# Batch 0's opening reordered, and eight PSUM banks for the first h phase, in a fused attention and Gelu MLP kernel

## Chip, core and metric

One core of a Trainium2 chip. The metric is the device time of one execution in microseconds (us); medians of several runs are given. The profile comes from one of these executions; its span is about 1.8 us shorter than the metric (279.0 for 280.8). In the lines, PE is TensorE, PEld its weight loads, ACT ScalarE, DVE VectorE and POOL GpSimd; the granted clock is the share of TensorE's full clock that it was given.

## The reference, cut to what matters

```python
# q, k, v: (8, 8, 576, 64) float32; w_in: (512, 2048); w_out: (2048, 512)
q_s = softmax(q, over d)                    # per row
k_s = softmax(k, over the sequence)
kv  = einsum('bhsd,bhse->bhde', k_s, v)     # 64 x 64 for each head
x   = einsum('bhsd,bhde->bhse', q_s, kv)    # -> (4608, 512)
h   = x @ w_in
out = gelu(h) @ w_out                       # Gelu with erf; (4608, 512) float32
```

Per batch ("chunk") the kernel makes 512 rows of x, then h = x·w_in in 16 tiles t of 128 columns (four matmuls each, one for each slice dm of x), Gelu, and y = g·w_out. The rest of each batch's rows form a ninth chunk.

## The kernel before: the parts concerned

PSUM has eight banks, in three pools: psum_h (three single banks), psum_y (two), psum_a (one single, tag "a", and one pair, tag "a2"). A pool hands its banks out in turn, and a bank comes free when its last reader has finished. The names in the profile lines: `eq` (shown as `e`) is exp(q), `qT` its transpose, `ek` exp(k), `v_aug` v in bfloat16 with a column of ones, `kvc` the normalised kv, `xT` x in bfloat16, `g` Gelu's output.

```python
    warm(5, zeros32)                     # matmuls with zeros, to have the PE clock up
    table(AF.Exp)
    exp_q(0, parts=2); exp_k(0, parts=2)
    norm_q(0, 0, 2)                      # first half: multiply on POOL
    norm_q(0, 1, 2, nc.vector)           # second half: multiply on DVE
    tp_mm(0, 0); tp_evac(0, 0, "s")      # "s": evacuated by ACT, else by DVE
    table(AF.Gelu)
    warm(2)
    cast_v(0, 0)                         # DVE
    for hp in range(1, HP): cast_v(0, hp, nc.gpsimd)
    cast_wi(0, wi[0], "p"); cast_wi(1, wi[1], "p")    # POOL
    tp_mm(0, 1)
    warm(2)
    # ... x_tile: x0, x1 in psum_y, x2 in psum_a, x3 in psum_h
    kv_mm(0, 0); kv_norm(0, 0, 1)        # kv of heads 0-3, then its normalisation on DVE
    tp_evac(0, 1)
    warm_x()
    x_mm(0, 0); x_evac(0, 0, "s"); x_evac(0, 1, "s")
    kv_mm(0, 1); kv_norm(0, 1, 2)        # kv of heads 4-7
    x_mm(0, 1); x_evac(0, 2); x_evac(0, 3, "s")
    h_phase(0, {...}, groups={0: 2, 4: 4, 8: 2}, ybanks=(6, 8))
```

`groups={4: 4}` computes tiles 4 to 7 side by side: dm is the outer loop, so a late slice of w_in is wanted later. `ybanks` are the tiles that take a psum_y bank. The kv tile of a batch, both halves in the same pair of banks:

```python
            st[b]["kv"] = psum_a.tile([128, 2, 2, 256], FP32, tag="a2", name="kv")
        # matmul into ps[c, i, half, 0:D + 1]: i picks the bank, half the columns in it
```

The softmax here doesn't subtract the row's maximum and nothing guards it: scores larger than these inputs give would overflow.

Of the kernel before, what the change touches and what calls it, by code (L numbers as in the profile page):

```python
# [8 lines left out]
FP32 = mybir.dt.float32  # L9
BF16 = mybir.dt.bfloat16  # L10
AF = mybir.ActivationFunctionType
# [5 lines left out]
def kernel(  # L17
# [16 lines left out]
    nc = tc.nc  # L34
# [4 lines left out]
    M = 128 * J  # L39
    R = S - M  # L40
    HP = H // 2
# [11 lines left out]
    psum_h = ctx.enter_context(tc.tile_pool(name="psum_h", bufs=3, space=bass.MemoryType.PSUM))  # L53
    psum_y = ctx.enter_context(tc.tile_pool(name="psum_y", bufs=2, space=bass.MemoryType.PSUM))
    psum_a = ctx.enter_context(tc.tile_pool(name="psum_a", bufs=1, space=bass.MemoryType.PSUM))
# [14 lines left out]
    zeros32 = singles.tile([128, 512], FP32)  # L70
    scr = singles.tile([128, 2], FP32)

    def setup_tiles():
        nc.vector.memset(scr, 0.0)
        for i in range(2):
            nc.vector.memset(v_aug[i][:, :, :, D:D + 1], 1.0)

    def table(func):
        nc.scalar.activation(out=scr[:, 1:2], in_=scr[:, 0:1], func=func)  # L79
# [76 lines left out]
    def cast_v(b, hp, eng=nc.vector):  # L156
        eng.tensor_copy(  # L157
            out=v_aug[b % 2][:, hp, :, 0:D],
            in_=st[b]["vf"][:, hp, :].rearrange("p (n d) -> p n d", n=NS),
        )  # L160
# [5 lines left out]
    def kv_mm(b, half):  # L166


        if "kv" not in st[b]:
            st[b]["kv"] = psum_a.tile([128, 2, 2, 256], FP32, tag="a2", name="kv")  # L170
        ps = st[b]["kv"]
        for n in range(NS):
            for i in range(2):
                for hh in range(2):
                    hp = 2 * half + i
                    pr = slice(hh * 64, hh * 64 + 64)
                    c = slice((hh ^ i) * 64, (hh ^ i) * 64 + 64)
                    nc.tensor.matmul(  # L178
                        ps[c, i, half, 0:D + 1], ek[b % 2][pr, hp, n, :],
                        v_aug[b % 2][pr, hp, n, 0:D + 1], start=(n == 0), stop=(n == NS - 1),  # L180
                    )

    def kv_norm(b, h0, h1):

        ps = st[b]["kv"]
        m = h1 - h0
        rec = small.tile([128, 2, 2], FP32, tag="reck")
        nc.vector.reciprocal(rec[:, :, 0:m], ps[:, :, h0:h1, D])
        nc.vector.tensor_tensor(  # L189
            out=kvc[b].rearrange("p (h i) d -> p i h d", i=2)[:, :, h0:h1],  # L190
            in0=ps[:, :, h0:h1, 0:D],
            in1=rec[:, :, 0:m].unsqueeze(3).to_broadcast([128, 2, m, D]), op=ALU.mult,
        )
# [21 lines left out]
    def tp_mm(b, half):  # L215
        if half == 0:
            st[b]["qT"] = attn_sb.tile([128, J, HP, 128], BF16, tag="qT", name="qT")
        if b == 1 and half == 1:
            ps = psum_a.tile([128, 2, J, 2, 128], BF16, tag="a2", name="tp")[:, 0]
        else:  # L220
            pool, tag = (psum_h, "h") if half == 1 else (psum_a, "a")
            ps = pool.tile([128, J, 2, 128], BF16, tag=tag)
        st[b][f"tp{half}"] = ps
        for i in range(2):
            hp = 2 * half + i
            for j in range(J):
                nc.tensor.transpose(  # L227
                    ps[:, j, i, :],
                    st[b]["eq"][:, j, 2 * hp:2 * hp + 2, :].rearrange("p h d -> p (h d)"),
                    identity,  # L230
                )

    def tp_evac(b, half, eng="v"):
        o = st[b]["qT"][:, :, 2 * half:2 * half + 2, :]
        if eng == "v":
            nc.vector.tensor_copy(out=o, in_=st[b][f"tp{half}"])
        else:
            nc.scalar.copy(out=o, in_=st[b][f"tp{half}"])  # L238
# [17 lines left out]
    def x_mm(b, half):  # L256

        for bb in range(B if b == B else 1):
            for r in range(2):
                for i in range(2):  # L260
                    hp = 2 * half + i
                    pr = slice(r * 64, r * 64 + 64)
                    c = slice((r ^ i) * 64, (r ^ i) * 64 + 64)
                    ps = st[b][f"x{hp}"]
                    if b < B:
                        nc.tensor.matmul(  # L266
                            ps[c, :], kvc[b][pr, hp, :], st[b]["qT"][pr, :, hp, :],
                            start=True, stop=True,
                        )
                    else:  # L270
                        nc.tensor.matmul(  # L271
                            ps[c, bb * R:(bb + 1) * R], kvc[bb][pr, hp, :],
                            st[b]["qT"][pr, bb // 2, hp, bb % 2 * R:(bb % 2 + 1) * R],
                            start=True, stop=True,
                        )
# [11 lines left out]
    def x_evac(b, hp, eng="v"):  # L287
        ps = st[b][f"x{hp}"]
        if eng == "v":
            nc.vector.tensor_copy(out=st[b]["xT"][:, hp, :], in_=ps)  # L290
        else:
            nc.scalar.copy(out=st[b]["xT"][:, hp, :], in_=ps)  # L292

    def h_phase(c, ins, groups={}, ybanks=()):


        g = moe_sb.tile([128, NDF, M], BF16, tag="g", bufs=1)
        st[c]["g"] = g
        xT = st[c]["xT"]
        t1 = 0  # L300
        while t1 < NDF:
            t0, t1 = t1, t1 + groups.get(t1, 1)
            ts = range(t0, t1)
            pss = []
            for t in ts:
                pool, tag = (psum_y, "y") if t in ybanks else (psum_h, "h")
                pss.append(pool.tile([128, M], FP32, tag=tag, name="ps"))
            for dm in range(NDM):
                for ps, t in zip(pss, ts):
                    nc.tensor.matmul(  # L310
                        ps, wi_bf[:, dm, t * 128:(t + 1) * 128], xT[:, dm, :],
                        start=(dm == 0), stop=(dm == NDM - 1),
                    )
            for ps, t in zip(pss, ts):
                nc.scalar.activation(out=g[:, t, :], in_=ps, func=AF.Gelu)  # L315
                for f in ins.get(t, []):
                    f()
# [68 lines left out]
    def cast_wi(i, w, eng):  # L386
        n = wi_cols[i]
        r = n // 128
        o = wi_bf[:, :, wi_off[i]:wi_off[i] + n].rearrange("p d (c m) -> p d c m", c=r)
        w = w[:, :, 0:n].rearrange("p d (m c) -> p d c m", c=r)  # L390
        if eng == "p":
            for h in range(2):
                nc.gpsimd.tensor_copy(out=o[:, 2 * h:2 * h + 2], in_=w[:, 2 * h:2 * h + 2])
        else:
            for c in range(NDM):
                nc.vector.tensor_copy(out=o[:, c], in_=w[:, c])  # L396
# [22 lines left out]
    def cast_wo(i, w, c0=0, n=4, eng="v"):  # L419
        o, w = wo_bf[:, 4 * i + c0:4 * i + c0 + n, :], w[:, c0:c0 + n]  # L420
        if eng == "v":
            nc.vector.tensor_copy(out=o, in_=w)  # L422
        else:
            nc.scalar.copy(out=o, in_=w)

    def warm(n, z=zeros):
        ps = psum_y.tile([128, DM], FP32, tag="y")
        for i in range(n):
            nc.tensor.matmul(ps, z[:, 0:128], z, start=True, stop=True)  # L429

    def warm_x():

        for r in range(2):
            for i in range(2):
                pr = slice(r * 64, r * 64 + 64)
                c = slice((r ^ i) * 64, (r ^ i) * 64 + 64)
                nc.tensor.matmul(
                    st[0][f"x{i}"][c, :], zeros[pr, 0:64], zeros[pr, :], start=True, stop=True,
                )
# [23 lines left out]
    nc.vector.memset(zeros32, 0.0)  # L463
    nc.vector.memset(zeros, 0.0)
    setup_tiles()
    warm(5, zeros32)


    table(AF.Exp)
# [3 lines left out]
    norm_q(0, 1, 2, nc.vector)  # L473
    tp_mm(0, 0)
    tp_evac(0, 0, "s")
    table(AF.Gelu)
    warm(2)
    cast_v(0, 0)
    for hp in range(1, HP):
        cast_v(0, hp, nc.gpsimd)  # L480
    cast_wi(0, wi[0], "p")
    cast_wi(1, wi[1], "p")
    tp_mm(0, 1)
    warm(2)
    for hp, pool, tag in ((0, psum_y, "y"), (1, psum_y, "y"), (2, psum_a, "a"), (3, psum_h, "h")):
        x_tile(0, hp, pool, tag)
    kv_mm(0, 0)
    kv_norm(0, 0, 1)
    tp_evac(0, 1)
    warm_x()  # L490
    x_mm(0, 0)
    x_evac(0, 0, "s")
    x_evac(0, 1, "s")
    kv_mm(0, 1)
    kv_norm(0, 1, 2)
    x_mm(0, 1)
    x_evac(0, 2)
    x_evac(0, 3, "s")
    h_phase(0, {
        0: [lambda: cast_wi(2, wi[2], "v")],  # L500
        2: [lambda: cast_wi(3, wi[3], "v")],
        6: [lambda: cast_wi(4, wi[4], "v")],
        9: [lambda: cast_wo(0, wo[0])],
        12: [lambda: cast_wo(1, wo[1])],
    }, groups={0: 2, 4: 4, 8: 2}, ybanks=(6, 8))


    exp_q(1, parts=2)
# [68 lines left out]
    for c in range(2, B + 1):  # L577
        nb = c + 2
        ins = {}
# [53 lines left out]
```

## Time and profile before

| | before |
|---|---|
| time, first three runs | 280.81 us (280.76 to 280.87) |
| PE's share of the chain that ended last | 93% |
| first transposes on PE | 9.98 us |
| kv of half 0 / of half 1 starts | 12.12 / 13.45 us |
| first h matmul (tile 0) | 14.92 us |
| first y matmul | 28.94 us |

Read the timeline from the first h matmul backwards. Everything after it is one nearly unbroken stream of matmuls, one every 0.216 us, so a change of the opening is worth what it moves that first matmul, plus the holes that it takes out of or puts into the stream. The lines themselves stand in the prediction. About one matmul in seventy is missing from the trace (1894 records, 1922 weight loads); such a gap is exactly two steps (0.432) and is no hole.

### The profile page before, as it was taken

What the parts mean: (1) busy time and instruction counts of PE and PEld (TensorE: products, weight loads), DVE (VectorE), ACT (ScalarE), POOL (GpSimd) and SP (SyncE); (2) the same over time, 40 slices, a digit from 0 to 9 for tenths busy, and PEclk for the clock granted to TensorE, in tenths of its full rate; (3) what the DMA queues carried; (4) which work ended last, traced back from release to release, by engine and by line L of the source; (5) the groups of instructions that cost most, each with busy time, mean ns of one, the idle gap of its engine ahead of it and who ended that gap; (6) DMA issues with size and microseconds to landing.
All of it is one profiled execution on the core that took longest, in us unless ns stands there. A gap on an engine that the chain in (4) does not pass through costs nothing.

```text
span 279.0 us, 4537 instructions
## 1 busy us (share of the span) xinstructions
PE 269.0 (96%) x1894; PEld 125.7 (45%) x1922; DVE 99.8 (36%) x151; ACT 158.0 (57%) x245; POOL 33.9 (12%) x26
## 2 busy tenths in 40 slices
PE   7689999999999999999999999999999999999995
PEld 3334454444444444444444444444444444444443
DVE  2766574309753530083007500651015200130012
ACT  4857766689377816691569346943683263136400
POOL 1720060002020130005000500050005000000000
PEclk9999999999999999999999999999999999999999
DMA  7999999962994139812991199117501500120033
GB/s 252 398 385 432 396 399 407 400 247 72 265 381 78 40 108 256 314 39 72 237 366 44 40 215 389 48 66 186 117 0 75 150 2 0 75 78 0 0 78 76
DMA packets 44980, 50.10 MB, mean 180 GB/s; under 512 B 20384, under 2 KB 29856, under 8 KB 44704
## 3 DMA queue, kind: packets, MB, share of 16 engines
q1 hardware_dynamic: 44560, 49.39, 53.5%
q10 hardware_dynamic: 400, 0.43, 0.5%
q8 instruction: 15, 0.25, 0.3%
q14 instruction: 5, 0.04, 0.1%
HBM read 36.70 MB, written 9.44 MB: 165 GB/s over the span
## 4 chain that ended last, share of the span: by engine, by line
PE 93%; DMA 2%; ACT 1%; issue 1%; POOL 1%; DVE 0%; SPq 0%
PE ps L310 45%; PE ps L320 43%; DMA f<-in_q_dram 2%; PE kv L178 2%; PE ps L266 2%; PE ps L345 1%; POOL e L210 1%; ACT L79 0%; ACT e L145 0%; PE ps L227 0%; ACT qT L238 0%; PE ps L271 0%; SPq L90 0%; PE tp L227 0%; PE xx L266 0%
## 5 line engine op out<-in xcount | busy, mean ns | idle before, releaser
L310 PE MATMUL ps<-xT,wi_bf 128*128 128x512 bf16 x565 | 125.6, 379 | 0.6
L320 PE MATMUL ps<-wo_bf,g 128*128 128x512 bf16 x543 | 122.1, 379 | 1.6 <-issue 1.1
L315 ACT ACTIVATE g<-ps 128x512 bf16<-128x512 f32 x144 | 85.2, 597 | 67.9 <-PE ps L310 67.8
L310 PEld LDWEIGHTS <-wi_bf 128*128 128x128 bf16 x576 | 56.1, 98 | 68.4 <-issue 1.1
L320 PEld LDWEIGHTS <-g 128*128 128x128 bf16 x560 | 54.0, 98 | 64.2 <-issue 0.4
L328 DVE COPY y_sb<-ps 128x512 f32<-128x512 f32 x34 | 23.2, 684 | 79.8 <-PE ps L320 76.8
L210 POOL TENSOR_TENSOR e<-e,recq 128x2048 bf16<-128x2048 bf16 (+1 forms) x9 | 25.7, 2856 | 177.8 <-DVE recq L209 143.0
L157 DVE CAST v_aug<-f 128x576 bf16<-128x576 f32 x25 | 17.1, 745 | 48.2 <-DMA f<-in_v_dram 48.2
L208 DVE TENSOR_REDUCE qsum<-e 128x16 f32<-128x1024 bf16 (+1 forms) x13 | 21.1, 1621 | 15.3 <-ACT e L145 15.2
L292 ACT CAST xT<-ps 128x512 bf16<-128x512 f32 x19 | 10.3, 589 | 26.5 <-PE ps L266 17.0
L145 ACT ACTIVATE e<-f 128x512 bf16<-128x512 f32 (+1 forms) x42 | 20.5, 556 | 2.9 <-DMA f<-in_q_dram 2.8
L150 ACT ACTIVATE ek<-f 128x2304 bf16<-128x2304 f32 (+1 forms) x10 | 17.1, 1726 | 0.4 <-DMA f<-in_k_dram 0.4
L290 DVE CAST xT<-ps 128x512 bf16<-128x512 f32 x15 | 9.7, 687 | 17.4 <-PE ps L266 14.6
L79 ACT ACT_TABLE_LOAD x9 | 11.5, 1283 | 2.8 <-issue 2.6
L429 PE MATMUL ps<-zeros 128*128 128x512 f32 (+1 forms) x14 | 8.0, 716 | 1.5 <-DVE zeros L463 1.5
L145 ACT ACT_TABLE_LOAD x7 | 9.0, 1283 | 0.1
L396 DVE CAST wi_bf<-w 128x512 bf16<-128x512 f32 x12 | 7.1, 623 | 2.1 <-DMA w<-in_moe_w_in_dram 1.7
L178 PEld LDWEIGHTS <-ek 64*64 64x64 bf16 x576 | 6.5, 105 | 2.5 <-ACT qT L238 0.4
L178 PE MATMUL kv<-v_aug,ek 64*64 64x65 bf16 x576 | 6.8, 193 | 0.0
L210 DVE TENSOR_TENSOR e<-e,recq 128x1024 bf16<-128x1024 bf16 x4 | 6.1, 1533 | 0.1
L266 PE MATMUL ps<-qT,kvc 64*64 64x512 bf16 x60 | 5.0, 390 | 1.0 <-DVE kvc L189 0.6
L422 DVE CAST wo_bf<-w 128x2048 bf16<-128x2048 f32 (+1 forms) x4 | 4.4, 1091 | 3.8 <-DMA w<-in_moe_w_out_dram 3.8
(37 smaller groups left out, 44.6 us busy)
## 6 DMA issues: line engine op xcount, KB each, us to landing
out_dram<-y_sb SPq DMA_DIRECT2D x32, 256.0 KB, 2.4
f<-in_k_dram SPq DMA_DIRECT2D x6, 1152.0 KB, 10.2
f<-in_v_dram SPq DMA_DIRECT2D x6, 1152.0 KB, 11.7
f<-in_q_dram SPq DMA_DIRECT2D x6, 1024.0 KB, 7.4
w<-in_moe_w_in_dram SPq DMA_DIRECT2D x6, 512.0 KB, 8.9
f<-in_v_dram SPq DMA_DIRECT2D x8, 288.0 KB, 6.8
f<-in_q_dram SPq DMA_DIRECT2D x4, 512.0 KB, 9.0
w<-in_moe_w_out_dram SPq DMA_DIRECT2D x2, 1024.0 KB, 12.2
```

Source lines behind the costliest of these rows:

```text
L79: nc.scalar.activation(out=scr[:, 1:2], in_=scr[:, 0:1], func=func)
L145: nc.scalar.activation(out=dst[:, i], in_=src[:, u], func=AF.Exp)
L150: nc.scalar.activation(out=ek[b % 2][:, i:i + n], in_=st[b]["kf"][:, i:i + n].rearrange("p x (n d) -> p x n d", n=NS), func=AF.Exp,)
L157: eng.tensor_copy(out=v_aug[b % 2][:, hp, :, 0:D], in_=st[b]["vf"][:, hp, :].rearrange("p (n d) -> p n d", n=NS),)
L178: nc.tensor.matmul(ps[c, i, half, 0:D + 1], ek[b % 2][pr, hp, n, :], v_aug[b % 2][pr, hp, n, 0:D + 1], start=(n == 0), stop=(n == NS - 1),)
L208: nc.vector.reduce_sum(out=qsum, in_=eq[:, :, hs, :], axis=AX.X)
L210: eng.tensor_tensor(out=eq[:, :, hs, :], in0=eq[:, :, hs, :], in1=recq.unsqueeze(3).to_broadcast([128, J, w, D]), op=ALU.mult,)
L266: nc.tensor.matmul(ps[c, :], kvc[b][pr, hp, :], st[b]["qT"][pr, :, hp, :], start=True, stop=True,)
L310: nc.tensor.matmul(ps, wi_bf[:, dm, t * 128:(t + 1) * 128], xT[:, dm, :], start=(dm == 0), stop=(dm == NDM - 1),)
L315: nc.scalar.activation(out=g[:, t, :], in_=ps, func=AF.Gelu)
L320: nc.tensor.matmul(ps, st[c]["g"][:, t, j * 128:(j + 1) * 128], wo_bf[:, t, :], start=(t == 0), stop=(t == NDF - 1),)
L328: nc.vector.tensor_copy(out=y_sb, in_=ps)
```

## The change

Its intent: have kv of both halves done before x, so that PE need not go back and forth between PE and DVE; give v's casts and the evacuations to the engines so that each piece is ready in turn; load Gelu's table when the last evacuation is done; and give the first h phase enough banks to compute tiles 4 to 7 and 8 to 11 side by side. `warm(7)` takes the place of `warm(5)`, and a later `warm(2)` goes.

```diff
@@ -463,7 +462,7 @@
     nc.vector.memset(zeros32, 0.0)
     nc.vector.memset(zeros, 0.0)
     setup_tiles()
-    warm(5, zeros32)
+    warm(7, zeros32)
 
 
     table(AF.Exp)
@@ -473,36 +472,51 @@
     norm_q(0, 1, 2, nc.vector)
     tp_mm(0, 0)
     tp_evac(0, 0, "s")
-    table(AF.Gelu)
     warm(2)
-    cast_v(0, 0)
-    for hp in range(1, HP):
-        cast_v(0, hp, nc.gpsimd)
+    cast_v(0, 0, nc.gpsimd)
+    cast_v(0, 1, nc.gpsimd)
+    cast_v(0, 2)
+    cast_v(0, 3, nc.gpsimd)
     cast_wi(0, wi[0], "p")
     cast_wi(1, wi[1], "p")
     tp_mm(0, 1)
-    warm(2)
+    tp_evac(0, 1, "s")
     for hp, pool, tag in ((0, psum_y, "y"), (1, psum_y, "y"), (2, psum_a, "a"), (3, psum_h, "h")):
         x_tile(0, hp, pool, tag)
     kv_mm(0, 0)
     kv_norm(0, 0, 1)
-    tp_evac(0, 1)
     warm_x()
+    kv_mm(0, 1)
+    kv_norm(0, 1, 2)
     x_mm(0, 0)
     x_evac(0, 0, "s")
-    x_evac(0, 1, "s")
-    kv_mm(0, 1)
-    kv_norm(0, 1, 2)
+    x_evac(0, 1)
     x_mm(0, 1)
-    x_evac(0, 2)
-    x_evac(0, 3, "s")
+    x_evac(0, 2, "s")
+    x_evac(0, 3)
+    table(AF.Gelu)
+
+    def ybank():
+        return psum_y.tile([128, M], FP32, tag="y", name="ps")
+
+    pair = []
+
+    def a2bank(i):
+        if not pair:
+            pair.append(psum_a.tile([128, 2, M], FP32, tag="a2", name="pair"))
+        return pair[0][:, i]
+
     h_phase(0, {
         0: [lambda: cast_wi(2, wi[2], "v")],
         2: [lambda: cast_wi(3, wi[3], "v")],
         6: [lambda: cast_wi(4, wi[4], "v")],
         9: [lambda: cast_wo(0, wo[0])],
         12: [lambda: cast_wo(1, wo[1])],
-    }, groups={0: 2, 4: 4, 8: 2}, ybanks=(6, 8))
+    }, groups={0: 2, 4: 4, 8: 4}, banks={
+        3: ybank, 6: ybank, 8: ybank,
+        9: lambda: psum_a.tile([128, M], FP32, tag="a", name="ps"),
+        10: lambda: a2bank(0), 11: lambda: a2bank(1),
+    })
 
 
     exp_q(1, parts=2)
```

The cut hunks replace the argument `ybanks` by `banks`, a map from a tile to a function that allocates its bank.

More of the change, by code (lines that the diff above doesn't have):

```diff
@@ L292, in x_evac, with h_phase @@
             nc.scalar.copy(out=st[b]["xT"][:, hp, :], in_=ps)
-    def h_phase(c, ins, groups={}, ybanks=()):
+    def h_phase(c, ins, groups={}, banks={}):
         g = moe_sb.tile([128, NDF, M], BF16, tag="g", bufs=1)
@@ L305, in h_phase @@
             for t in ts:
-                pool, tag = (psum_y, "y") if t in ybanks else (psum_h, "h")
-                pss.append(pool.tile([128, M], FP32, tag=tag, name="ps"))
+                pss.append(banks[t]() if t in banks else psum_h.tile([128, M], FP32, tag="h", name="ps"))
             for dm in range(NDM):
```

## The prediction

> **What bounds the kernel now.** I read the page first (busy shares, clock row, chain by line), then the timelines of each engine over the first 45 us, then the waits.
>
> ```profile
> PE 269.0 (96%) x1894; PEld 125.7 (45%) x1922; DVE 99.8 (36%) x151; ACT 158.0 (57%) x245; POOL 33.9 (12%) x26
> PEclk9999999999999999999999999999999999999999
> PE 93%; DMA 2%; ACT 1%; issue 1%; POOL 1%; DVE 0%; SPq 0%
> ```
>
> The reader is to see that TensorE (PE) holds 93% of the chain that ended last, at full clock. The change touches only the opening, before batch 0's first matmul with w_in, and the first h phase. All else it can do is let the same stream of matmuls start earlier or lose a hole, so the gain is at most a few us of 280.81. The timelines (columns: start, duration, engine, line, operation, tiles, shapes, count, idle before and releaser) show the opening:
>
> ```profile
> 9.98 0.62 PE L227 MATMUL ps<-identity,e 128*128 128x128 bf16 x8 [1.71 <-POOL e L210]
> 11.15 0.61 PE L227 MATMUL ps<-identity,e 128*128 128x128 bf16 x8
> 12.12 0.48 PE L178 MATMUL kv<-v_aug,ek 64*64 64x65 bf16 x36
> 13.21 0.41 PE L266 MATMUL ps<-qT,kvc 64*64 64x512 bf16 x4 [0.40 <-ACT scr L79]
> 14.58 0.41 PE L266 MATMUL ps<-qT,kvc 64*64 64x512 bf16 x4 [0.62 <-DVE kvc L189]
> 14.92 14.19 PE L310 MATMUL ps<-xT,wi_bf 128*128 128x512 bf16 x62
> ...
> 11.67 1.28 ACT L79 ACT_TABLE_LOAD   x1
> ...
> 12.87 0.29 DVE L189 TENSOR_TENSOR kvc<-kv,rec 128x128 bf16<-128x128 f32 x1
> ...
> 9.54 1.46 DVE L210 TENSOR_TENSOR e<-e,recq 128x1024 bf16<-128x1024 bf16 x1
> 10.93 0.74 DVE L157 CAST v_aug<-f 128x576 bf16<-128x576 f32 x1
> 8.02 1.90 POOL L210 TENSOR_TENSOR e<-e,recq 128x1024 bf16<-128x1024 bf16 x1 [6.71 <-ACT e L145]
> 10.41 2.34 POOL L157 CAST v_aug<-f 128x576 bf16<-128x576 f32 x3 [0.49 <-DMA f<-in_v_dram]
> 13.23 2.58 POOL L393 CAST wi_bf<-w 128x512 bf16<-128x512 f32 x4 [0.48 <-DMA w<-in_moe_w_in_dram]
> ```
>
> From 9.98 to 14.92 PE does little and waits on short chains: transposes of q, kv of half 0, its normalisation, x of half 0, then the same for half 1. The h phase starts at 14.92 and the y phase at 28.94: 64 tile-steps in 14.02 us. The wait "ACT scr L79" is a coincidence of ends: the table's dummy activation ends at 12.96 + 0.20, kvc at 12.87 + 0.29, both 13.16, and kvc is what x needs. There is one true hole inside the h phase:
>
> ```profile
> 15.58 1.03 PE L310 MATMUL ps<-xT,wi_bf 128*128 128x512 bf16 x4
> ...
> 18.38 1.22 PE L310 MATMUL ps<-xT,wi_bf 128*128 128x512 bf16 x4
> ...
> 18.58 0.60 ACT L315 ACTIVATE g<-ps 128x512 bf16<-128x512 f32 x1 [0.27 <-PE ps L310]
> ```
>
> Four matmuls take 1.03 at the steady pace (three steps of 0.216 and a last one of 0.379) and 1.22 here. The fourth is w_in tile 7's first. Counting the psum_h rotation (three buffers: transposes, x3, tiles 0, 1, 2, 3, 4, 5, 7), tile 7 takes tile 3's bank, whose Gelu ends at 18.58 + 0.60 = 19.18. The hole is 0.19 us.
>
> **What the Trainium skill says.** "GPSIMD Engine Reference", section 8, says that GpSimd shares its SBUF interfaces with VectorE and contends with DVE instructions that have two SBUF inputs. The trace agrees: DVE's normalising multiply took 1.46 us beginning at 9.54, while POOL's ran until 9.92, but 1.23 in a later place where they hardly overlap; and POOL's three v casts take 2.34 us at 10.41 where three take 2.06 at 38.83. I read it as turns: DVE's multiply works from 9.92 to 11.00, and a POOL cast given before that gets going only at 11.00.
>
> "PSUM — Partial Sum Buffer", section "PSUM bank collisions raise a hardware error", says two engines may not touch one bank in the same partitions at once and that hardware does not arbitrate, so software must order them. The kv tile holds half 0 and half 1 in the same two banks. That such ordering is in this program, even wider, by whole tile, is suggested here:
>
> ```profile
> 45.51 0.69 DVE L290 CAST xT<-xx 128x512 bf16<-128x512 f32 x1 [0.20 <-PE xx L266]
> 46.23 0.59 ACT L292 CAST xT<-xx 128x512 bf16<-128x512 f32 x1 [0.82 <-DVE xT L290]
> ```
>
> ACT reads the other half of one PSUM tile only after DVE has finished.
>
> "ScalarE: Activation LUTs", section "What ACT_TABLE_LOAD costs", gives about 1283 ns plus a drain of about 1380. The trace shows 1.28 and 0.20 for the dummy call, and no such drain: I use 1.48.
>
> **The change part by part.**
>
> 1. *warm(7) for warm(5).* Ten passes end at 1.45 + 6.82 = 8.27. Later passes step by about 0.43, so four more add 1.7 us and end at 9.98, the last one's successor being issuable at about 9.4. The transposes wait for POOL until 9.98. Cost 0.
>
> 2. *v casts.* v0, v1, v3 go to POOL, v2 to DVE. POOL is free at 9.92 instead of 10.41 (it no longer waits for v1's landing), but the port belongs to DVE until 11.00. v0 then ends near 11.53, v1 near 12.14, v3 near 12.75: just when POOL's three ended before (10.41 + 2.34 = 12.75). kv of half 0 needs v0 and v1, so it starts at 12.14 + 0.04 = 12.18, against 12.12. The warm(2) taken out stood in a gap that the casts now leave anyway. Worth −0.06 (a loss).
>
> 3. *kv of half 1 ahead of x.* From kv's start to the end of kvc took 12.12 to 13.16, 1.04 us; so kvc half 0 is ready at 13.23. By the bank rule kv of half 1, which writes those banks, waits for it: it starts at 13.26 and its kvc is ready at 14.30. x of half 0 is issued behind it at about 13.6 and seen done 0.45 later, 14.06. ACT evacuates x0 from 14.07 to 14.66 (its 0.59). DVE evacuates x1 behind kvc, 14.23 to 14.92 (0.69). x of half 1 waits for kvc, 14.35, seen done 14.80; x2 on ACT to 15.40, x3 on DVE to 15.53.
>
> 4. *Start of the h phase.* Tiles 0 and 1 are a pair, each needing a slice of x every 0.43 us. PE is past x of half 1 at 14.35 + 0.34 = 14.70 (14.58 to 14.92 before), x0 is there at 14.66, the first w_in cast (13.23 plus half of 1.3) long before. So h starts at 14.70, and x1 (needed 15.13), x2 (15.56), x3 (16.00) are in time. Worth 14.92 − 14.70 = 0.22.
>
> 5. *tp_evac of half 1 on ACT* costs 1.01 there instead of 0.68 on DVE; it runs 11.79 to 12.80, before anything waits. 0.
>
> 6. *Gelu's table last*: 15.41 to 16.9 on ACT. Tile 0's sum is ready at about 16.4, so the first Gelu moves from 16.64 to 16.88. Its bank is wanted by tile 4 at 14.70 + 16 × 0.216 = 18.15; it is free at 17.5. 0.
>
> 7. *Banks.* Tile 3 moves to psum_y, so tile 7 gets tile 2's bank. Tile 2's Gelu ends at about 18.46; tile 7 starts at 14.70 + 19 × 0.216 = 18.80. The hole of 0.19 goes. Tiles 8 to 11 get four free banks. Their weights are cast by DVE between 19.85 and 22.3, paced by landings; side by side their slices are wanted at 21.6, 22.5, 23.3 and 24.2, singly somewhat sooner, but in time as well. So the four-wide group removes no wait of this trace; 0. Tile 12 and the y banks look free in time by 0.2 us or more. Worth 0.2.
>
> Sum: 0.22 + 0.2 = 0.42. It is carried on: in chunk 1's front end the tightest landing is w_out's row cast on ACT, 40.82 + 0.62 = 41.44, for matmuls at 42.43 − 0.42. Behind it nothing but PE's own work sets the end. 280.81 − 0.42 = 280.39.
>
> **The rivals.**
>
> *kv of half 1 does not wait for kvc of half 0.* Then it starts when v3 is cast, 12.80; kvc half 1 is ready at 13.84, x of half 1 at 13.89, h at 14.36 (bound by x0's evacuation), and the gain is 0.56 + 0.2 = 0.76: 280.05. For it: different columns. Against: same banks, and the xx lines above. I give it 15%.
>
> *A late transfer takes the gain back.* w_in's later casts end at 19.85 + 4.89 = 24.74; tile 12's last slice is wanted at about 25.7. The DMA queues do not move, since the wst buffers are freed by landings and casts as before. If I have mis-sized one, up to all of the 0.42 returns as a wait: 280.8. I give it 10%.
>
> *The clock drops.* "TensorE: Matmul & The Clock Gate", Part 1, has the clock halve after about 3.4 us of idleness. Before, the gap from 8.27 to 9.98 did no harm here; after, the gaps are shorter than 0.6 us each though frequent. A window at half clock would cost over a us: 281.5 to 282. I give it 3%.
>
> *POOL keeps the port* and casts v0 before DVE's multiply. Then the second transposes come at 11.75, kv still waits for v1: no change.
>
> **Range and chances.** 85% on 0.42 and 15% on 0.76 average 0.47, so 280.35. Eight in ten: 279.95 to 280.7; the low end is the first rival with a little more, the high end a chain step of 0.3 us lost. Runs of before agree to 0.1 us. Two per cent is 5.6 us, which the opening cannot give or take: faster 0.005, same 0.985, slower 0.01.
>
> **What would show it.** Kv of half 1 on PE at about 13.26, directly behind kvc's end, or at 12.80 if the rival holds; first h matmul at 14.70; no hole at tile 7; y phase at about 28.5; a constant lead in every later chunk. Kv of half 0 well before 12.1 would refute the port reading; an h start later than 14.9 or a new hole at tile 8 or 12 would make the prediction wrong.

## The result, and the profile after

The changed kernel took 280.31 us in the median (280.13 to 280.37, six runs); the kernel before 280.79 (280.76 to 282.01, six). That is 0.48 us less, inside the range and at 0.04 from the point. The ratio, computed as the mean time of one kernel's fast runs over that of the other's of the same rounds (so not quite the ratio of the medians), is 0.9975, interval 0.9958 to 0.9991: the same at 2%. It is lower than the ratio of the medians (280.31 / 280.79 = 0.9983), because one run of the kernel before took 282.01. That run turned out to matter; see the warming experiments.

PE's timeline of the changed kernel (start, duration, engine, line, operation, tiles, shapes, count, idle time before and who ended it):

```profile
10.01 0.62 PE L227 MATMUL ps<-identity,e 128*128 128x128 bf16 x8
11.72 0.22 PE L178 MATMUL kv<-v_aug,ek 64*64 64x65 bf16 x2
12.22 0.47 PE L178 MATMUL kv<-v_aug,ek 64*64 64x65 bf16 x34 [0.28 <-POOL v_aug L157]
13.29 0.48 PE L178 MATMUL kv<-v_aug,ek 64*64 64x65 bf16 x36 [0.38 <-DVE kvc L189]
13.58 0.41 PE L266 MATMUL ps<-qT,kvc 64*64 64x512 bf16 x4
14.38 0.41 PE L266 MATMUL ps<-qT,kvc 64*64 64x512 bf16 x4 [0.39 <-DVE kvc L189]
14.72 7.51 PE L309 MATMUL ps<-xT,wi_bf 128*128 128x512 bf16 x33
...
28.54 2.75 PE L319 MATMUL ps<-wo_bf,g 128*128 128x512 bf16 x12
```

The h phase starts 0.20 us earlier (14.72 for 14.92) although kv of half 0 is later (12.22 for 12.12, but for its first two matmuls): it waits for POOL's cast of v1. Kv of half 1 stands idle 0.38 us until DVE has normalised half 0. The y phase comes 0.40 earlier (28.54 for 28.94), so another 0.20 was won inside the h phase. The other engines of the changed kernel, in the same columns:

```profile
12.94 0.29 DVE L189 TENSOR_TENSOR kvc<-kv,rec 128x128 bf16<-128x128 f32 x1
...
9.90 2.88 POOL L157 CAST v_aug<-f 128x576 bf16<-128x576 f32 x3
...
15.43 1.28 ACT L79 ACT_TABLE_LOAD   x1
16.84 2.14 ACT L314 ACTIVATE g<-ps 128x512 bf16<-128x512 f32 x4
```

DVE's kvc of half 0 ends at 12.94 + 0.29 = 13.23, and kv of half 1 starts 0.06 behind it. POOL began its casts 0.5 us earlier than before (9.90 for 10.41) and ended them at 12.78 (before: 12.75): the head start bought nothing. And the hole: these are the four matmuls of the changed kernel whose last is tile 7's first.

```profile
18.18 1.03 PE L309 MATMUL ps<-xT,wi_bf 128*128 128x512 bf16 x4
```

1.03 us, for 1.22 before: the steady pace, and no hole. Sum: 0.20 + 0.20 = 0.40, which is also the difference of the two profiled spans (279.0 and 278.6). The medians differ by 0.48; the other 0.08 is within the spread of the runs.

### The profile page after: what moved, and what is told of

Same layout as the page of the kernel before. It is cut to its first block, busy times and chain, and to the rows that moved or that the text cites. A ratio compares the mean times of both kernels' runs of the same rounds, so it can differ in the third digit from the quotient of the medians.

```text
span 278.6 us, 4542 instructions
## 1 busy us (share of the span) xinstructions
PE 270.3 (97%) x1896; PEld 126.4 (45%) x1924; DVE 100.1 (36%) x151; ACT 157.8 (57%) x245; POOL 34.4 (12%) x26
## 4 chain that ended last, share of the span: by engine, by line
PE 93%; DMA 2%; POOL 1%; DVE 1%; issue 1%; ACT 0%; POOLq 0%
PE ps L309 44%; PE ps L319 43%; PE kv L178 2%; DMA f<-in_q_dram 2%; PE ps L266 1%; PE ps L344 1%; POOL v_aug L157 1%; POOL e L210 1%; PE pair L309 1%; ACT e L145 0%; DVE qsum L208 0%; PE ps L271 0%; DVE kvc L189 0%; PE tp L227 0%; PE ps L227 0%
## 5 line engine op out<-in xcount | busy, mean ns | idle before, releaser
L309 PE MATMUL ps<-xT,wi_bf 128*128 128x512 bf16 x557 | 124.3, 379 | 0.6
L314 ACT ACTIVATE g<-ps 128x512 bf16<-128x512 f32 x142 | 83.7, 597 | 66.9 <-PE ps L309 66.9
L290 DVE CAST xT<-ps 128x512 bf16<-128x512 f32 x16 | 10.3, 686 | 17.0 <-PE ps L266 14.1
L428 PE MATMUL ps<-zeros 128*128 128x512 f32 (+1 forms) x16 | 9.1, 728 | 1.5 <-DVE zeros L462 1.5
L428 PEld LDWEIGHTS ps<-zeros 128*128 128x128 f32 x14 | 3.5, 256 | 5.7 <-issue 4.3
L157 POOL CAST v_aug<-f 128x576 bf16<-128x576 f32 x7 | 5.6, 811 | 2.3 <-DMA f<-in_v_dram 2.2
```

The lines of the kernel that those rows point to most:

```text
L157: eng.tensor_copy(out=v_aug[b % 2][:, hp, :, 0:D], in_=st[b]["vf"][:, hp, :].rearrange("p (n d) -> p n d", n=NS),)
L309: nc.tensor.matmul(ps, wi_bf[:, dm, t * 128:(t + 1) * 128], xT[:, dm, :], start=(dm == 0), stop=(dm == NDM - 1),)
L314: nc.scalar.activation(out=g[:, t, :], in_=ps, func=AF.Gelu)
L428: nc.tensor.matmul(ps, z[:, 0:128], z, start=True, stop=True)
```

## The experiments

Theory: the change gains by the kv order (h phase earlier) and by tile 3's bank (hole gone); the v deal costs; the four-wide group and the table's place are worth nothing. Each variant undoes or does one part. Every group of runs was timed on one chip beside the kernel before: 280.83 in the first group, 280.75 in the second, 280.83 and 280.77 in the last two. The changed kernel itself was timed in the first comparison only, on another occasion than its variants; the kernel before, whose medians differ by 0.08 at most, ties the groups together, so a difference of medians across groups is good to about 0.1 us, and the smaller ones below rest on the traces. The opening's absolute times shift by 0.1 or 0.2 us from run to run with the first transfers (first transposes at 9.80 to 10.06 in most), so I also compare the distance from the first transposes to the first h matmul: 14.92 − 9.98 = 4.94 before, 14.72 − 10.01 = 4.71 after. The first transposes wait for POOL's multiply of exp(q) and begin about 0.06 us behind its end; in some profiles the warming matmuls held them longer, which is said where it matters.

### Tile 3's bank alone

```diff
-    }, groups={0: 2, 4: 4, 8: 2}, ybanks=(6, 8))
+    }, groups={0: 2, 4: 4, 8: 2}, ybanks=(3, 6, 8))      # kernel before
```

> The kernel before with one thing of the change: w_in tile 3 in a psum_y bank. My theory: the hole at tile 7 goes (four matmuls around 18.4 us take 1.03 us instead of 1.22), the h phase still starts at about 14.92 and the y phase at 28.75 instead of 28.94; time 0.2 us below the kernel before (some 280.6). Rival, that the whole gain came of the earlier start of the h phase and the hole would have moved elsewhere: 0.0, y phase at 28.94.

Measured: 280.55 (280.48 to 280.65), 0.28 under the median of the kernel before. Its timeline:

```profile
18.23 1.24 PE L310 MATMUL ps<-xT,wi_bf 128*128 128x512 bf16 x5
...
28.81 2.54 PE L320 MATMUL ps<-wo_bf,g 128*128 128x512 bf16 x11
```

Five matmuls in 1.24 us (four steps of 0.216 and 0.379) with tile 7's first as the fifth: no hole. The h phase began at 14.98 and lasted 13.83, against 14.02 before. One number added to a tuple is worth 0.2 us of the whole; the rival falls.

### The four-wide group undone

```diff
-    }, groups={0: 2, 4: 4, 8: 4}, banks={
-        3: ybank, 6: ybank, 8: ybank,
-        9: lambda: psum_a.tile([128, M], FP32, tag="a", name="ps"),
-        10: lambda: a2bank(0), 11: lambda: a2bank(1),
+    }, groups={0: 2, 4: 4, 8: 2}, banks={
+        3: ybank, 6: ybank, 8: ybank,
     })
```

> The changed kernel without the four-wide group of tiles 8 to 11 (pair 8-9, then singles, as before; tile 3 stays in psum_y). My theory: no wait at w_in's second half existed, so y phase still at 28.54 and time as the changed kernel (280.3), difference under 0.05 us. Rival, that the four-wide group hides late casts or Gelu waits: a new hole of 0.1 us or more between 21.6 and 25 us and a later y phase.

Measured: 280.28 (280.13 to 280.40), for 280.31; h phase at 14.69, y phase at 28.51, 13.82 us apart as in the changed kernel. The group of four and its extra banks are worth nothing here. No wait for a slice of w_in shows in either.

### x of half 0 ahead of kv of half 1 again

```diff
+    x_mm(0, 0); x_evac(0, 0, "s"); x_evac(0, 1, "s")
     kv_mm(0, 1); kv_norm(0, 1, 2)
-    x_mm(0, 0); x_evac(0, 0, "s"); x_evac(0, 1)
-    x_mm(0, 1); x_evac(0, 2, "s"); x_evac(0, 3)
+    x_mm(0, 1); x_evac(0, 2); x_evac(0, 3, "s")
```

> The changed kernel with x of half 0 again ahead of kv of half 1, and x's evacuations on the engines as before. My theory: putting both kv first is what brought the h phase forward; undone, x of half 0 starts at 13.28, kv of half 1 at 13.5, its kvc ends at 14.6 and the h phase starts at about 15.0 instead of 14.72: 0.28 us slower than the changed kernel, some 280.6. Rival, that the order is worth nothing because kv of half 1 waits for kvc of half 0 anyway: h phase within 0.1 us of 14.72, time 280.3.

Measured: 280.53 (280.45 to 280.75), 0.25 above the variant before it in the same group and 0.22 above the changed kernel. Its first transposes were early (9.80) and its h phase at 14.79: the distance is 4.99, for 4.71. So the order gives 0.28 in distance, as expected, in spite of the wait between the halves: kv of half 1 is issued right behind half 0's normalisation, not behind x of half 0 as well, and its own normalisation ends that much sooner.

### v's casts dealt as before

```diff
-    cast_v(0, 0, nc.gpsimd)
-    cast_v(0, 1, nc.gpsimd)
-    cast_v(0, 2)
-    cast_v(0, 3, nc.gpsimd)
+    cast_v(0, 0)
+    for hp in range(1, HP): cast_v(0, hp, nc.gpsimd)
```

> The changed kernel with v's casts dealt as before (v0 on DVE, v1 to v3 on POOL). My theory of turns at the shared port: POOL's first cast cannot work before 11.03 in either deal, so the new deal delays kv of half 0 from some 11.8 to 12.22; undone, kv of half 0 is complete-able at 11.8, kvc half 0 ends near 12.8, kv of half 1 starts near 12.84 and the h phase at about 14.26 instead of 14.72: 0.46 us faster than the changed kernel, some 279.85. Rival, that the deal was needed (kv of half 1 then waits for v3 and the x evacuations set h): gain 0 to 0.1 or a loss.

Measured: 280.04 (279.87 to 280.11), 0.27 below the changed kernel; the direction is right, the size was put at 0.46. The change's own deal of v's casts was a loss. Its timeline:

```profile
10.72 2.15 POOL L157 CAST v_aug<-f 128x576 bf16<-128x576 f32 x3 [0.92 <-DMA f<-in_v_dram]
...
11.60 0.48 PE L178 MATMUL kv<-v_aug,ek 64*64 64x65 bf16 x36
12.78 0.62 PE L178 MATMUL kv<-v_aug,ek 64*64 64x65 bf16 x36 [0.48 <-ACT qT L238]
```

Kv of half 0 comes at 11.60, 1.74 us behind the first transposes (9.86), for 2.21 after: 0.47, all that was expected. Then half of it is lost. In this execution v landed later (POOL idle 0.92 for it), v3's cast ended at 10.72 + 2.15 = 12.87, and kv of half 1 stretched over that (0.62 for 0.48). The h phase starts at 14.34, a distance of 4.48, for 4.71: 0.23. A second profile with this deal, `v_deal_x_banks` below, bears this out: there v landed sooner, the casts ended at 10.15 + 2.45 = 12.60, kv of half 1 took 0.48, and the distance is 14.18 − 9.85 = 4.33, a gain of 0.38. (The releaser that the last line names, ACT's second evacuation, ended at 12.69, close behind the normalisation of half 0 at 12.34 + 0.29 = 12.63. Kv does not read qT, and in `v0_on_act` below kv of half 1 began at 12.75 with that evacuation running until 12.77, so the name is probably a coincidence of ends.) My expectation had used the landing of one earlier run: in seven profiles where v1 is POOL's first cast, it begins, on landing, anywhere between 10.15 and 10.72.

### Kv's halves in separate banks

The normalisation of half 1 then takes four DVE instructions, since its two tiles are no longer one:

```diff
+        if b == 0 and half == 1:
+            st[b]["kv1"] = [psum_h.tile([128, M], FP32, tag="h", name="kv1") for i in range(2)]
...
-                        ps[c, i, half, 0:D + 1], ek[...
+                        (kv1[i][c, 0:D + 1] if b == 0 and half == 1 else ps[c, i, half, 0:D + 1]), ek[...
```

x3 is allocated behind it, in the bank of the second transposes.

> The changed kernel with kv of half 1 of batch 0 in two psum_h banks of its own (x3 takes the bank of the second transposes; the normalisation of half 1 is four DVE instructions instead of two). My theory, that kv of half 1 stands waiting for DVE's reading of half 0 only since both halves share banks: kv of half 1 starts at v3's cast, some 12.82 in place of 13.29, its kvc ends at about 14.05 in place of 14.32, the h phase starts at about 14.45: 0.27 us faster than the changed kernel, some 280.05. Rival, that another wait (v3's cast, or the order of the engines) holds it anyway: within 0.1 us of 280.3.

Measured: 279.97 (279.89 to 280.10), 0.34 below the changed kernel, a little more than expected. PE's lines:

```profile
12.69 0.58 PE L180 MATMUL kv<-v_aug,ek 64*64 64x65 bf16 x36
14.35 7.50 PE L321 MATMUL ps<-xT,wi_bf 128*128 128x512 bf16 x34
```

Kv of half 1 starts at 12.69, with no wait for DVE in front (half 0's kvc ended at 12.92 + 0.29 = 13.21 in this run), and the h phase at 14.35, although this run's first transposes came late, at 10.47: the seven warming matmuls ran until 1.45 + 9.18 = 10.63 here, past POOL's multiply, which had ended at 9.92. So the 0.38 us that PE stood before kv of half 1 in the changed kernel came of what the halves share, and of nothing else. This variant gives half 1 a tile as well as banks of its own, so it does not tell whether the tile or the banks are what is kept in order. The program orders the accesses; no instruction of the source asks for it.

### v0's cast on ACT

```diff
-    cast_v(0, 0, nc.gpsimd)
...
     exp_k(0, parts=2)
+    nc.scalar.copy(out=v_aug[0][:, 0, :, 0:D], in_=st[0]["vf"][:, 0, :].rearrange(...))
```

> The changed kernel with v0's cast on ACT, between the second exp of k and the first evacuation of the transposes, v1 and v3 on POOL, v2 on DVE. My theory of turns at the port: ACT does not share it, v0 is cast by about 10.75, v1 by 11.55, v3 by its landing plus 0.7, so kv of half 0 is complete at about 11.65 and kvc half 0 at 12.7; the h phase starts near 14.2 in place of 14.72, if w_in's first cast on POOL (landing plus 0.7, 13.8 to 14.2 in the runs so far) is in time: 0.4 to 0.5 us faster than the changed kernel, some 279.85. Rival, that ACT's later evacuation of the transposes or the landings give it back: 280.0 or more.

Measured: 280.01 (279.90 to 280.15), 0.30 below the changed kernel. That is less than the 0.4 to 0.5 that I expected, and at the rival's mark (280.0 or more). The profile shows kv of half 0 at 11.66 and the h phase at 14.18, as expected (distance 14.18 − 10.01 = 4.17). The start is 0.54 earlier than in the changed kernel, and so is the y phase (28.00 for 28.54); but the last matmul is only 0.41 earlier. The rest was given back in batch 1's front end. PE there, and ACT with the cast of a row of w_out:

```profile
41.08 0.48 PE L178 MATMUL kv<-v_aug,ek 64*64 64x65 bf16 x36
41.64 1.02 PE L319 MATMUL ps<-wo_bf,g 128*128 128x512 bf16 x4
...
40.97 0.62 ACT L423 CAST wo_bf<-w 128x512 bf16<-128x512 f32 x1 [1.39 <-DMA w<-in_moe_w_out_dram]
```

The matmuls with that row start 0.56 behind kv; in the variant with all mends, below, it is 0.41 (41.07 and 41.48), since there the row was cast from 40.38 on. Here the row landed later, its cast ended at 41.59, and PE waited for it: 0.15 us. This is the tightest landing that the prediction named when it carried its sum on, and what its rival of a late transfer describes. In the changed kernel's profile that cast ended at 40.37 + 0.62 = 40.99, and PE did not wait for it. Three lines show the port again:

```profile
9.43 1.54 DVE L210 TENSOR_TENSOR e<-e,recq 128x1024 bf16<-128x1024 bf16 x1
...
10.45 1.05 POOL L157 CAST v_aug<-f 128x576 bf16<-128x576 f32 x1 [0.56 <-DMA f<-in_v_dram]
11.85 0.67 POOL L157 CAST v_aug<-f 128x576 bf16<-128x576 f32 x1 [0.35 <-DMA f<-in_v_dram]
```

and one of the changed kernel:

```profile
9.90 1.66 POOL L157 CAST v_aug<-f 128x576 bf16<-128x576 f32 x1
```

A cast of the same shape on POOL takes 1.05 us when DVE's multiply runs until 10.97, and 0.67 afterwards; in the changed kernel, whose multiply ran until 11.04, the first one took 1.66. In all 14 profiles POOL's first cast ended 0.52 or 0.53 us after DVE's multiply, whether it had begun 0.16 or 1.14 us before that end, and DVE's multiply ended 1.07 to 1.09 us after POOL's own, wherever it had begun between 9.23 and 9.57. That is what turns look like; two engines that only slowed each other would hardly end at fixed distances. ACT's cast of v0 took 0.65 beside the same multiply.

### Batch 1's x2 and x3 in separate tiles, with the v deal of before

The hole near 46 us is in both kernels. In the kernel before it is here (four matmuls in 1.20, not 1.03):

```profile
46.04 1.20 PE L310 MATMUL ps<-xT,wi_bf 128*128 128x512 bf16 x4
```

```diff
+    x_tile(1, 2, psum_a, "a")
     xx = psum_a.tile([128, 2, M], FP32, tag="a2", name="xx")
-    st[1]["x2"], st[1]["x3"] = xx[:, 0], xx[:, 1]
+    st[1]["x3"] = xx[:, 1]
```

> The changed kernel with v's casts dealt as before, and batch 1's x2 and x3 in separate PSUM tiles (x2 in psum_a's single bank). My theory that a PSUM tile is ordered as a whole: ACT's evacuation of x3 no longer waits 0.8 us for DVE's of x2, the hole of some 0.18 us near 46.1 goes, and the time is 0.18 below that of the deal of before alone (280.04): some 279.86. Rival, that the wait seen on ACT was for something else: the hole stays, 280.04.

Measured: 279.85 (279.62 to 280.14), for 280.04 without this edit in the other group: 0.19 less, or 0.11 when each is taken against the kernel before of its own group (280.75 and 280.83). The lines of its profile:

```profile
44.55 0.69 DVE L290 CAST xT<-ps 128x512 bf16<-128x512 f32 x1 [0.20 <-PE xx L266]
44.59 0.59 ACT L292 CAST xT<-xx 128x512 bf16<-128x512 f32 x1
...
45.32 1.24 PE L309 MATMUL ps<-xT,wi_bf 128*128 128x512 bf16 x5
```

ACT reads x3 beside DVE's reading of x2, 0.04 us apart, where it waited 0.82 before; and the stretch where the hole was runs at the steady pace (five in 1.24); the variant without this edit still has four in 1.20 there. The two tiles' halves lie in different banks, so here the order of the program was wider than the banks ask for.

### Gelu's table where it was

```diff
     tp_evac(0, 0, "s")
+    table(AF.Gelu)
...
     x_evac(0, 3)
-    table(AF.Gelu)
```

> The changed kernel with Gelu's table loaded where it was, behind the first evacuation of the transposes. My theory: ACT's second evacuation then ends at about 14.2 in place of 12.84, x0's follows it and ends at 14.78 in place of 14.61, the h phase starts about 0.1 us later (14.8): 280.4. The first Gelu comes earlier, at about 16.5, and nobody waits for it. Rival, that the table in front of the first Gelu costs time: 280.1 or less.

Measured: 280.34 (280.17 to 280.69), for 280.31: no difference to be seen. The first part of the chain is as expected: the second evacuation of the transposes ends at 13.14 + 0.99 = 14.13, and x's evacuations follow; but the h phase starts at 14.67, not at the 14.8 that I expected. (Its distance of 4.61 flatters it, since the transposes were held until 10.06 by the warming matmuls; from the end of POOL's multiply it is 4.80, for 4.77 in the changed kernel.) The place of the table is worth nothing that can be seen, neither way. There is no drain beside the 1.28 and 0.20 us.

### Five warming matmuls, then three

```diff
-    warm(7, zeros32)
+    warm(5, zeros32)      # and in another variant: warm(3, zeros32)
```

> The changed kernel with five warming matmuls at the start as before, not seven. My theory: the two more are neither on the path nor needed for the clock, since the gap before the first transposes did no harm in the kernel before: transposes of 56 ns a step and h phase at 14.7 all the same, 280.3. Rival, that the thinner matmuls after it now let the clock fall: steps of 107 ns or more and matmuls of 0.43 us in the opening, over a us slower.

Measured: median 280.45, with 280.20 to 280.91 in five runs and 282.49 in the sixth, the profiled one. (The run of 280.91 has a lowered clock too, 0.994.) My theory of "not needed for the clock" fell on this run. The clock row of its page and one stretch (columns: stretch, length, busy time and count of PE, weight loads, DVE, ACT, POOL, then granted clock, DMA share, GB/s):

```profile
PEclk9869999999999999999999999999999999999999
...
10.00:18.70 8.70, 8.01 (x111) 3.79 (x112) 6.18 (x12) 4.82 (x7) 5.19 (x7) 0.61 1.06 381
```

and the changed kernel in the same stretch:

```profile
10.00:18.70 8.70, 7.47 (x121) 3.90 (x122) 6.17 (x12) 6.48 (x11) 5.23 (x7) 1.00 1.06 398
```

From 10 to 18.7 us the granted clock was 0.61 of full, against 1.00. PE had stood idle for 2.32 us before this run's first transposes, for 1.71 in the profiled run of the kernel before; the transposes themselves still took 0.62 us, and the clock fell between 11 and 12 us. So I formed a new theory and tested it with fewer still.

> The changed kernel with three warming matmuls at the start, not seven. My new theory, after the profile of the variant with five fell into a stretch at half clock (10 to 18.7 us) and no run of a kernel with seven has: PE idle ahead of the first transposes sets how often the clock falls. With three the idle time grows to some 3.5 to 4 us, so most of the six runs are slow: 281.5 to 284. Rival, that the slow runs come by chance and have nothing to do with the warming: at most one of six, median 280.3.

Measured: 281.11 (280.79 to 281.29). All six runs have a mean granted clock of 0.988 or 0.994 in the records, where undisturbed runs have 0.997 to 1.000. The loss is smaller than I expected (0.5 to 1.0 us over the changed kernel, not 1.2 to 3.7), as the clock came back sooner in its profile:

```profile
PEclk9599999999999999999999999999999999999999
...
9.89 1.03 PE L227 MATMUL ps<-identity,e 128*128 128x128 bf16 x8 [4.00 <-POOL e L210]
```

PE had been idle for 4.00 us, and the transposes then took 1.03 us for 0.62. Over all runs: of ten kernels with seven warming matmuls, 60 runs, none had a mean clock under 0.997 or a time over 280.8. The kernel before, with five, had a run of 281.7 us or more in 9 of 50; the records of eight of these show a clock of 0.994. (For the ninth, in the first comparison, I have the time alone.) `tile3_alone`, with five as well, had none in six. Fewer warming matmuls change two things, the idle time before the transposes and the work done before it; the runs do not separate them.

### All mends together

v0 on ACT, kv's halves apart, x2 and x3 apart, as in the diffs above; and the same without the separate kv banks.

> The changed kernel with three mends together: v0's cast on ACT, kv of half 1 of batch 0 in banks of its own, batch 1's x2 and x3 in separate PSUM tiles. My theory: the mends overlap. With v0 on ACT kv of half 1 could start at v3's cast, some 12.55, only 0.2 us ahead of kvc half 0, and the two more DVE instructions take 0.15 of it; w_in's first cast on POOL (13.8 to 14.2) is then the next bound. The h phase at 14.1, the hole of 0.18 near 46 gone: 279.8. Rival, that the gains add up (0.3 + 0.33 + 0.18 off 280.31): 279.5.

> The changed kernel with v0's cast on ACT and batch 1's x2 and x3 in separate PSUM tiles, kv's halves in shared banks as in the change. My theory: 280.01 (v0 on ACT alone) less the hole of 0.18: 279.83, within 0.1 of all three mends together. Rival, that the shared banks still cost: 0.2 us or more above all three.

Measured: all three 279.67 (279.36 to 279.83), ratio to the kernel before 0.9948 (0.9931 to 0.9965); without separate kv banks 279.93 (279.73 to 280.09). All three beat the changed kernel by 0.64 us, and the kernel before by 1.16. The sum of the three gains over the changed kernel is 0.83 by the medians as they stand (0.30, 0.34, 0.19) and 0.67 with each against the kernel before of its own group (0.26, 0.30, 0.11), for 0.64 or 0.68 measured: the medians do not settle whether they overlap. The two variants, timed together, are 0.26 apart where I expected 0.1, which is the mark of the second one's rival: what kv's halves share still costs. PE's lines of all three:

```profile
13.98 7.70 PE L321 MATMUL ps<-xT,wi_bf 128*128 128x512 bf16 x34
27.99 3.19 PE L331 MATMUL ps<-wo_bf,g 128*128 128x512 bf16 x14
...
PEld L321 <- POOL wi_bf L404: 0.2, 1, 0.2
```

The h phase starts at 13.98, the earliest of all, and at once loses 0.2 us to a new wait: the cast of w_in on POOL (last line, from the view of the waits: 0.2 us, once). The other variant starts at 14.17 and reaches its y phase at 27.99 too. So in this execution of all three the transfer of w_in and its cast took over as the bound; the other variant lost nothing there, and the two profiled runs (279.60 and 279.73) do not show the 0.26 us between the medians. Landings differ from run to run, and w_in's and w_out's are now close to PE's needs; where the other executions won or lost their time is not shown.

## Why the prediction was right

Step by step, in its own numbering:

1. *warm(7), "Cost 0".* Right for the profiled run, whose transposes began at 10.01, 0.06 behind POOL, and for the time of a fast run (five warming matmuls: 280.2 to 280.5 in four of the runs). But its margin was misread: about 9.4 is where the last pass itself starts, so its successor can start only a step of 0.43 later, at about 9.83, and the slack was some 0.15 us. In the profile of the separate kv banks the passes ended later and held the transposes by about 0.5; there the wait for v1's cast hid it. **Wrong by omission**: it is the one part that acts on the slow runs. The prediction had the rival the wrong way round: it gave 3% to the clock falling after the change, where the kernel before is the one that suffers it, and said that "the gap from 8.27 to 9.98 did no harm here". It did none in the profiled execution. In 9 of 50 runs the kernel before was 0.9 us or more slower, eight of them at a lower recorded clock. That is why the ratio of the means is below that of the medians. That these falls sit in the opening is shown by one profile each for the variants with five and three, and only inferred for the kernel before.
2. *v casts, a loss of 0.06.* Kv of half 0 at 12.22 in place of 12.12: a loss of 0.10. The reading of turns at the port held (v0 cast by 9.90 + 1.66 = 11.56, predicted 11.53; the last cast by 12.78, predicted 12.75). What the step missed is that the old deal gives 0.27 more under the new order. In the kernel before, v0 and v1 were cast by 11.67, and kv of half 0 came at 12.12 because `warm(2)` (at 11.59) stood in front of it; the change took that out, and lost the gain by giving v0 to POOL.
3. *Kv of half 1 waits for kvc of half 0.* Predicted 13.26, 13.29 measured; x of half 0 13.6 and 13.58; x of half 1 14.35 and 14.38. The rival without this wait, 280.05, is what separate banks gave (279.97), so the step was the right one to hang the choice on.
4. *h phase at 14.70.* 14.72.
5. and 6. *Evacuation on ACT and the table: 0.* The evacuation ran until 12.84, predicted 12.80, with nothing waiting for it; no variant tests it alone. Predicted first Gelu 16.88, measured 16.84; moving the table back made no difference.
7. *Banks, 0.2, and 0 for the group of four.* Both confirmed alone: 0.2 us of hole for tile 3, nothing for the group.

The predicted 280.39 by the sum and 280.35 after weighing met 280.31. Most of this is no luck, since the times inside the opening agree within 0.05 us step by step; that the medians came within 0.04 is, as they stray by more than that between groups. The expectations written later were worse in places: they took landings as fixed, which they are not.

## What to carry to other kernels

When one engine sets the end, follow its stream backwards to the first instruction that waits and count buffers in the order of allocation: a hole of 0.2 us was one bank taken in the wrong rotation, and the four-wide group with its extra banks beside it was worth nothing. Look for accesses that the program orders because two pieces share a PSUM bank or tile, and split the tile before you reorder the work. And look at the spread of runs, not only at the median: warming matmuls that cost nothing in the fast runs can be what keeps the slow ones away.

## What the Trainium skill lacked or had wrong

- "ScalarE: Activation LUTs", section "What ACT_TABLE_LOAD costs": it adds a drain of about 1380 ns to the load of about 1283. Here the load took 1.28 us, the next activation began 0.02 us behind it (15.43 + 1.28 = 16.71, then 16.73 in the changed kernel), and the load itself 0.01 behind the evacuation before it (14.83 + 0.59 = 15.42); no such drain shows.
- "TensorE: Matmul & The Clock Gate", Part 1, has the clock fall after an idle window of about 3.4 us. Here less was enough in the two profiles that caught a fall. With three warming matmuls the clock is 1.00 from 6 to 8 us, 0.55 from 8 to 9 and 0.50 from 9 to 10, so it fell at about 8.1 (an estimate from these figures), some 2.2 us after the last of them (1.45 + 4.44 = 5.89). With five it fell between 11 and 12 us (0.82, then 0.50), when PE had stood idle for 2.32 us at most and had been at work again since 9.97.
- No page that I used says that whole PSUM tiles, not only banks, are kept in order in such a program: of two engines reading different banks of one tile, the second waited 0.82 us for the first; with two tiles they began 0.04 us apart.
